# First 32 heads of a sliding-window attention and feed-forward kernel: head pairs on halves of the matrix array, a new step table

## The chip, the cores and the metric

One core of a Trainium2 chip. The metric is the device time of one execution in microseconds (us); of several runs the median counts. A profile is one further execution, with the hardware profiler on.

## The reference

Attention over 4 batches, 8 heads, 768 rows and 64 columns, in which a row sees the last 128 keys and the first 4 ("sinks"), then a feed-forward layer of 3072 tokens:

```python
keep = is_sink | in_window                      # window 128, n_sink 4
scores = np.where(keep, scale * (q @ k.T), -1e9)
a = softmax(scores)
x = (a @ v).transpose(0, 2, 1, 3).reshape(3072, 512)
h = x @ w_in                                    # 512 -> 2048
out = (h * np.cos(h)) @ w_out                   # 2048 -> 512
```

Inputs are fp32; the result must be close to fp32 exactness.

## The kernel before

**Dense part.** The 3072 tokens are cut into six dense pairs of 512 rows, and each pair into 16 slots of 128 hidden columns. A slot is two half products `h_pair` (L476, 12 matmuls of 128x512), the cosine factor on ACT (`half_sine`, `square`) and DVE (`gate_square`, L498, called the gate below), a split of the result into a high and a low part (`g_hi` ACT L507, `g_lo` DVE L514), and `out_pair` (L523, 12 matmuls). Every fp32 product is three matmuls of high and low parts. The last accumulator of the last pair is scaled in two halves, one on ACT (L543), one on DVE (L545).

**Weights.** The arrays come with 64 bits per element. 32 pieces of 512 KB are loaded into two `raw` buffers, and each is put together on DVE by three operations (shift L595, top L601, low L607), rounded on ACT (L628), and its rest is taken on DVE (L631).

**Attention.** Heads 0 to 31 are *early*: the first 256 rows of each batch for 8 heads, in true fp32 matmuls, which the profile records twice each. For two heads at a time q and k are loaded (`load_natural`, L947), transposed on PE into `qk` (L955) and copied out. Before, q went into `early`, where each head's 64 rows are followed by zeros on the other 64 partitions, by two copies of 64x256, so that each head's scores (L992) contract over all 128 partitions. The mask (DVE L1070) and the exponential (ACT L1079) follow, `norm` (L1099, L1097) divides, the probabilities are transposed (`tp`, L1170) and copied (L390 on ACT, L392 on DVE). The values (L1215) multiply by a V that is padded with 64 zero columns, so that two heads are added into one bank. For heads 0 to 15 the sum is split into `xhi` (ACT L349) and `xlo` by a matmul that subtracts (`x_minus`, L354) and a copy. Heads 0 to 15 are done before the first dense slot; heads 16 to 31 and all *late* heads (32 to 95, high and low parts, L1048 scores, L1239 values) lie between dense slots.

**What sets the order.** Class `Plan` takes each step with its engines, duration, dependences and a wished time made from the table `C`, and writes one in-order list per engine. A step with more engines goes to one of them by the same table. `FILL` matmuls without use (L1556, `idle`) are put in where the plan sees PE idle ahead of the first dense matmul. Loads go through SP's queue, two weight pieces and the two scalars through ACT's.

Of the kernel before, what the change touches and what calls it, by code (L numbers as in the profile page):

```python
# [11 lines left out]
I32 = mybir.dt.int32  # L12
# [7 lines left out]
GR = 96 + 2 * NSINK  # L20
# [11 lines left out]
    "POOLF": 0.999, "POOLPEN": 2.492, "R": 2, "RAW": 2, "SAME": 0.056, "SEM": 0.352, "SPE": -0.019, "STEP": 7.601,  # L32
# [140 lines left out]
def attn_moe_kernel(ctx, tc, q, k, v, n_sink, window, w_in, w_out, out):  # L173
# [51 lines left out]
    neg, quarter = neg3[:, 0:2], neg3[:, 2:3]  # L225
# [7 lines left out]
    def setup():  # L233

        nc.scalar.dma_start(out=nw_i[:, 0, :], in_=n_sink.unsqueeze(0))
        nc.scalar.dma_start(out=nw_i[:, 1, :], in_=window.unsqueeze(0))
        nc.gpsimd.memset(ident, 0.0)
# [5 lines left out]
        nc.gpsimd.iota(rc_i[:, 1], pattern=[[1, P]], base=0, channel_multiplier=0)  # L243
        nc.vector.memset(ones, 1.0)
# [11 lines left out]
        nc.vector.tensor_copy(out=rc, in_=rc_i)  # L256
        nc.vector.tensor_single_scalar(out=env.below, in_=rel, scalar=0.0, op=ALU.is_lt)
# [94 lines left out]
    def x_minus(y, p, cs):  # L352
        def fn(e):
            nc.tensor.matmul(  # L354
                out=y.f(p, cs), lhsT=minus, rhs=xhi[:, p, cs], start=False, stop=True, skip_group_check=True
            )
        return fn

    def x_lo(y, p, cs, early):
        def fn(e):  # L360
            if early:
                copy(e, xlo[:, p, cs], y.f(p, cs))
            else:
                e.tensor_tensor(out=xlo[:, p, cs], in0=y.f(p, cs), in1=f32(xhi)[:, p, cs], op=ALU.subtract)
        return fn

    def split_early(plan, x, y, p, t):

# [3 lines left out]
        m = add([("PE", 0.12)], x_minus(y, p, cs), [i], t + 0.3)  # L372
        env.minus.users.append(m)
        j = add([("ACT", act(NT, False)), ("DVE", dve(NT))], x_lo(y, p, cs, True), [m], t + 0.6)
        y.parts[p] += [i, j]
        return [i, m, j]

    def split_late(plan, y, p, t):

        add = plan.add  # L380
        cs = slice(0, PT)
        i = add([("ACT", act(PT))], x_hi(y, p, cs), [k for x in y.xs for k in x.sums[p]] + [y.bx[p // 2]], t)
        j = add(sub(PT), x_lo(y, p, cs, False), [i, y.bx[p // 2]], t + 0.3, port=True)
        y.parts[p] += [i, j]
        for b in y.bf[p // 2]:
            b.users += [i, j]
# [151 lines left out]
    def out_half(y, j, half):  # L538
        def fn(e):
            y.o[j] = f32(raws[y.bo[j].nth]).rearrange("p n w -> p (n w)")[:, :DM]  # L540
            cs = slice(half * DM // 2, (half + 1) * DM // 2)
            if e is nc.scalar:
                e.activation(out=y.o[j][:, cs], in_=y.acc[j][:, cs], func=AF.Copy, scale=-2.0)  # L543
            else:
                e.tensor_single_scalar(out=y.o[j][:, cs], in_=y.acc[j][:, cs], scalar=-2.0, op=ALU.mult)  # L545
        return fn

# [13 lines left out]
    def sub(n):  # L561
        return (("POOL", 0.16 + n * 2.08e-3), ("DVE", dve(n)))
# [198 lines left out]
    def dense_pair(plan, y, s, t, T, w_in_ready, w_out_ready, banks, h_bank):  # L761
# [25 lines left out]
        for j in range(NJ):  # L787
            d = [a5, a6] + w_out_ready[s] + (accs[j].users[:1] or [accs[j]])
# [7 lines left out]
        for j in range(NJ):  # L796
# [7 lines left out]
            elif j < NJ - 1:  # L804
                i = [add(c[:1], out_scaled(y, j, other), d, c0 + 10.0)]
            else:
                i = [add([(e, w / 2)], out_half(y, j, n), d, c0 + 10.0) for n, (e, w) in enumerate(c)]
# [12 lines left out]
    def banded_path(ctx2):  # L820
# [33 lines left out]
        def x1r():  # L854

            if env.x1r is None:
                env.x1r = ap.tile([P, NP * NT], F32R, name="x1r", tag="x1")
                env.vs = env.x1r.rearrange("p (a b c d) -> p a b c d", a=NP, b=2, c=2)
            return env.x1r

        def sink_values():
            x1r()
# [13 lines left out]
        def load_batch_v(o):  # L876
            def fn(e):
                o.vs32 = xb[:, : 2 * D].rearrange("p (n d) -> p n d", d=D)
                for h in range(4):
                    for dup in range(2):  # L880
                        r0 = h * 32 + dup * 8
                        nc.sync.dma_start(
                            out=o.vs32[r0 : r0 + 8], in_=v[o.b, h::4, 0:NSINK, :].rearrange("p s d -> s p d")
                        )
# [36 lines left out]
        def load_v(o):  # L921
            def fn(e):
                if o.early:
                    o.vp = env.vp[o.odd]
                    o.v32 = o.vp[:, :, o.odd * D : o.odd * D + D]
                else:
                    o.v32 = v32s[:, o.bxv.nth, : o.nkb]
# [3 lines left out]
                )  # L931
            return fn
# [9 lines left out]
        def load_natural(tile, src, n):  # L942

            def fn(e):
                dst = tile.rearrange("p a b -> p (a b)")[:, : n * 2 * D].rearrange("p (n h d) -> p n h d", n=n, d=D)
                for h in range(2):
                    nc.sync.dma_start(out=dst[:, :, h, :], in_=src(h).rearrange("(n s) d -> s n d", s=P))  # L947
# [19 lines left out]
        def early_q(e):  # L967
            env.early = ap.tile([P, 2, 4 * P], F32, name="early", tag="ph")
            env.tqe = env.early[:, 1].rearrange("p (a n) -> p a n", a=2)
            for odd in range(2):  # L970
                e.memset(env.tqe[64 - odd * 64 : 128 - odd * 64, odd], 0.0)

        def early_v(e):
            env.vp = [
                ap.tile([P, CB, 2 * D], F32, name="vpe", tag="vr"),
                v32_t[:, : CB * 2 * D].rearrange("p (n d) -> p n d", d=2 * D),
            ]
            e.memset(env.vp[0][:, :, D:], 0.0)
            e.memset(env.vp[1][:, :, :D], 0.0)

        def k_out(o):
            def fn(e):
                o.tk = ap.tile([P, o.nkb, o.sw], F32, name=f"tk_{o.tag}", tag="tk")
                copy(e, o.tk.rearrange("p n s -> p (n s)"), o.qk[:, 1, : o.nkb * P])
            return fn

        def scores_pe(o, oe, j):
            def fn(e):
                i, w = o.i0 + j, o.ws[j]
                o.s_ps[j] = ps.tile([P, BW], F32, name=f"s_{o.tag}_{j}", tag=o.s_tag[j])  # L990
# [890 lines left out]
```

## Time and profile before

| | |
|---|---|
| runs | 724.87, 725.13, 725.80 us, median 725.13 |
| profiled execution | 727.14 us |
| its span, first to last instruction | 725.3 us |
| PE, DVE, ACT, POOL busy | 98%, 83%, 73%, 18% |
| mean granted clock of PE | 0.998 |
| first dense matmul | 57.08 us |
| gate of slot 0, gate of slot 16 | 69.74 us, 190.75 us |
| last weight subtraction (L631) | 160.0 us |

Busy means that an instruction of the engine is in progress. Matmuls overlap: a dense matmul is recorded with some 390 ns, but the next starts 230 ns after it, so starts tell more than busy times.

### The profile page before, as it was taken

What the parts mean: (1) busy time and instruction counts of PE and PEld (TensorE: products, weight loads), DVE (VectorE), ACT (ScalarE), POOL (GpSimd) and SP (SyncE); (2) the same over time, 40 slices, a digit from 0 to 9 for tenths busy, and PEclk for the clock granted to TensorE, in tenths of its full rate; (3) what the DMA queues carried; (4) which work ended last, traced back from release to release, by engine and by line L of the source; (5) the groups of instructions that cost most, each with busy time, mean ns of one, the idle gap of its engine ahead of it and who ended that gap; (6) DMA issues with size and microseconds to landing.
All of it is one profiled execution on the core that took longest, in us unless ns stands there. A gap on an engine that the chain in (4) does not pass through costs nothing.

```text
span 725.3 us, 12983 instructions
## 1 busy us (share of the span) xinstructions
PE 707.8 (98%) x3674; PEld 583.6 (80%) x3674; DVE 599.3 (83%) x1850; ACT 527.3 (73%) x1344; POOL 127.0 (18%) x213
## 2 busy tenths in 40 slices
PE   7888999999999999999999999999999999999997
PEld 6766787888888888888888888888888888888885
DVE  6889999998988978988978989888988875567763
ACT  3796886787797697796686886877887856566652
POOL 1010000000333222232231232232122322100000
PEclk9999999999999999999999999999999999999999
DMA  5665565533255333355433254533244410375651
GB/s 144 177 181 162 140 178 148 155 67 66 63 118 130 86 67 54 64 125 128 93 58 59 42 144 101 122 63 62 44 124 107 111 35 12 96 198 158 167 138 63
DMA packets 236500, 77.11 MB, mean 106 GB/s; under 512 B 221060, under 2 KB 221060, under 8 KB 236420
## 3 DMA queue, kind: packets, MB, share of 16 engines
q1 hardware_dynamic: 236128, 75.15, 43.5%
q10 hardware_dynamic: 292, 1.05, 0.5%
q8 instruction: 31, 0.51, 0.3%
q14 instruction: 49, 0.40, 0.2%
HBM read 69.86 MB, written 6.29 MB: 105 GB/s over the span
## 4 chain that ended last, share of the span: by engine, by line
PE 78%; ACT 12%; DVE 5%; issue 2%; DMA 2%; SPq 0%; ACTq 0%; DVEq 0%
PE h L476 30%; PE acc L523 30%; PE av L1239 4%; PE s L1048 4%; ACT p L1079 3%; PE s L992 2%; PE tp L1160 2%; PE av L1215 2%; DMA xk<-in_k_dram 2%; ACT p L1097 1%; ACT L485 1%; ACT L1079 1%; PE qk L955 1%; PE tp L1170 1%; ACT early L390 1%
## 5 line engine op out<-in xcount | busy, mean ns | idle before, releaser
L523 PE MATMUL acc<-whi_out,ghi 128*128 128x512 f32 x376 | 158.7, 422 | 0.0
L476 PE MATMUL h<-xhi,whi_in 128*128 128x512 f32 x384 | 155.3, 405 | 0.0
L476 PE MATMUL h<-xlo,whi_in 128*128 128x512 f32 x384 | 150.9, 393 | 0.0
L476 PE MATMUL h<-xhi,wlo_in 128*128 128x512 f32 x384 | 150.1, 391 | 0.0
L523 PE MATMUL acc<-whi_out,glo 128*128 128x512 f32 x376 | 147.8, 393 | 0.0
L523 PE MATMUL acc<-wlo_out,ghi 128*128 128x512 f32 x376 | 147.1, 391 | 0.0
L1198 POOL TENSOR_SCALAR_AFFINE_SELECT ph<-ph 128x512 fp32r<-128x512 f32 x128 | 87.2, 681 | 230.9 <-DVE ph L1191 227.1
L485 ACT ACTIVATE r<-h 128x512 f32<-128x512 f32 x96 | 57.1, 598 | 47.9 <-PE h L476 45.3
L476 PEld LDWEIGHTS h<-xlo,whi_in 128*128 128x128 f32 x384 | 72.1, 188 | 16.2
L523 PEld LDWEIGHTS acc<-whi_out,glo 128*128 128x128 f32 x376 | 70.6, 188 | 15.8
L476 PEld LDWEIGHTS h<-xhi,whi_in 128*128 128x128 f32 x384 | 72.3, 188 | 12.0 <-DVE r L498 0.3
L476 PEld LDWEIGHTS h<-xhi,wlo_in 128*128 128x128 f32 x384 | 72.5, 189 | 11.3
L523 PEld LDWEIGHTS acc<-whi_out,ghi 128*128 128x128 f32 x376 | 71.4, 190 | 10.4
L1079 ACT ACTIVATE p<-p,st 128x136 f32<-128x136 f32 (+1 forms) x192 | 79.3, 415 | 0.3
L523 PEld LDWEIGHTS acc<-wlo_out,ghi 128*128 128x128 f32 x376 | 71.3, 190 | 9.2
L498 DVE SCALAR_TENSOR_TENSOR r<-r,h 128x512 f32<-128x512 f32 x96 | 64.5, 674 | 16.9 <-ACT r L491 16.3
L507 ACT CAST ghi<-r 128x512 fp32r<-128x512 f32 x94 | 58.2, 619 | 19.6 <-PE acc L523 12.7
L514 DVE TENSOR_TENSOR glo<-r,ghi 128x512 fp32r<-128x512 f32 x94 | 65.3, 694 | 5.6 <-ACT ghi L507 4.9
L1070 DVE CUSTOM_DVE_ANT_0 p<-s,mk 128x136 f32<-128x136 f32 (+1 forms) x192 | 59.7, 313 | 6.2 <-PE s L992 2.8
L1008 ACT CAST l<-tq 64x256 fp32r<-64x256 f32 x64 | 25.8, 403 | 46.9 <-PE s L1048 46.4
L1056 DVE COPY_PREDICATED s<-mk,s 128x128 f32<-128x128 int32 x128 | 37.2, 291 | 25.6 <-PE s L1048 23.7
L1048 PEld LDWEIGHTS s<-r,l 128*128 128x128 f32 x256 | 46.4, 188 | 12.3 <-DVE ph L1191 1.4
(161 smaller groups left out, 1314.7 us busy)
## 6 DMA issues: line engine op xcount, KB each, us to landing
xk<-in_k_dram SPq DMA_DIRECT2D x256, 48.0 KB
raw<-in_moe_w_out_dram SPq DMA_DIRECT2D x16, 512.0 KB
wt<-in_moe_w_in_dram SPq DMA_DIRECT2D x32, 256.0 KB
raw<-in_moe_w_in_dram SPq DMA_DIRECT2D x14, 512.0 KB
v<-in_v_dram SPq DMA_DIRECT2D x64, 96.0 KB
raw<-in_v_dram SPq DMA_DIRECT2D x32, 192.0 KB
out_dram<-wt SPq DMA_DIRECT2D x22, 256.0 KB
wt<-in_moe_w_out_dram SPq DMA_DIRECT2D x20, 256.0 KB
```

The source lines that it names most:

```text
L476: nc.tensor.matmul(out=o.h, lhsT=w[:, c, fs], rhs=xx[:, c, :], start=(c == 0 and n == 0), stop=(c == NC - 1 and n == 2),)
L485: nc.scalar.activation(out=o.r, in_=o.h, func=AF.Sin, scale=0.5)
L498: nc.vector.scalar_tensor_tensor(out=o.r, in0=o.r, scalar=0.5, in1=o.h, op0=ALU.subtract, op1=ALU.mult)
L507: nc.scalar.copy(out=o.ghi, in_=o.r)
L514: e.tensor_tensor(out=o.glo, in0=o.r, in1=f32(o.ghi), op=ALU.subtract)
L523: nc.tensor.matmul(out=y.acc[j], lhsT=gg[:, j * P : (j + 1) * P], rhs=w[:, f, :], start=(f == 0 and n == 0), stop=(f == NFT - 1 and n == 2),)
L1048: nc.tensor.matmul(out=o.s_ps[j][:, :w], lhsT=o.l[:, j * P : (j + 1) * P], rhs=r.rearrange("p n s -> p (n s)")[:, c0 : c0 + w], start=(n = ...
L1056: nc.vector.copy_predicated(out=o.s_ps[j][:, :P], mask=below.bitcast(I32), data=o.s_ps[j][:, SW : SW + P])
L1070: nc.vector.tensor_tensor_reduce(out=o.pj[j][:, :w], in0=o.s_ps[j][:, :w], in1=masks[min(o.i0 + j, 2)][:, :w], op0=ALU.add, op1=ALU.min, s ...
L1079: nc.scalar.activation(out=o.pj[j][:, :w], in_=o.pj[j][:, :w], func=AF.Exp, bias=o.lead.st[:, 0, o.nth, j : j + 1], scale=-1.0, accum_out= ...
L1198: nc.gpsimd.affine_select(out=ph[:, :, b, :], in_=f32(ph)[:, :, 1, :], pattern=[[0, 2 * CB], [(-1, 1)[b], P]], compare_op=(ALU.is_gt, ALU. ...
L1239: nc.tensor.matmul(out=dst, lhsT=lhs, rhs=rhs, start=(n == 0), stop=(n == len(seq) - 1), skip_group_check=True)
```

## The change

- **Scores.** One step per pair of heads: q of both heads lies on 128 partitions (one copy of 128x256), and each head's matmul contracts over its own 64 partitions and row half of the array, into a bank of its own. The four matmuls of a pair stand together, the two heads in turn.
- **Values.** One step per pair: V has 64 columns per head, and each head's matmul uses one column half of the array, into its own half of the partitions of one bank. The zero fills of `early` and V are gone.
- **Split.** `x_minus` is gone; `xlo` is a DVE subtraction of 128x256.
- **Start.** q of the first two heads is loaded ahead of all weights on SP's queue, k on ACT's; the first two weight pieces follow, one on each queue.
- **Sinks.** The sink columns of four late heads are spread to 64 columns; the sink rows of V come by 8 broadcast loads of 32 partitions per batch instead of 8 of 8, and take three DVE operations per head group instead of two.
- **Others.** The two halves of the last accumulator are one operation on ACT. q, k and V of the early pairs have two buffers each. A subtraction of over 256 columns may no longer go to POOL.
- **Table.** Every constant of `C` that shapes the order is new; `FILL` is 110 instead of 60, `WARM` 3 instead of 5.

```diff
-    "L": 1, "LAG": 3.569, "LEAD": 43.095, "NM": 3.042, "NW": 2.459, "NWF": 0.527, "PB": 5, "PEN": 23.912,
+    "L": 1, "LAG": 2.866, "LEAD": 31.596, "NM": 0.567, "NW": 2.085, "NWF": 1.648, "PB": 5, "PEN": 132.787,
...
-        nc.scalar.dma_start(out=nw_i[:, 0, :], in_=n_sink.unsqueeze(0))
+        nc.sync.dma_start(out=nw_i[:, 0, :], in_=n_sink.unsqueeze(0))
         nc.scalar.dma_start(out=nw_i[:, 1, :], in_=window.unsqueeze(0))
+        for e, load in zip((nc.sync, nc.scalar), env.boot):
+            load(e)
...
-        for raw, src in env.first:
-            nc.scalar.dma_start(out=raw.rearrange("p n w -> p (n w)"), in_=src)
+        for e, (raw, src) in zip((nc.scalar, nc.sync), env.first):
+            e.dma_start(out=raw.rearrange("p n w -> p (n w)"), in_=src)
...
-    def x_lo(y, p, cs, early):
-        def fn(e):
-            if early:
-                copy(e, xlo[:, p, cs], y.f(p, cs))
-            else:
-                e.tensor_tensor(out=xlo[:, p, cs], in0=y.f(p, cs), in1=f32(xhi)[:, p, cs], op=ALU.subtract)
+    def x_lo(y, p, cs):
+        def fn(e):
+            e.tensor_tensor(out=xlo[:, p, cs], in0=y.f(p, cs), in1=f32(xhi)[:, p, cs], op=ALU.subtract)
...
-        def q_out(o, odd):
-            def fn(e):
-                r = slice(odd * 64, odd * 64 + 64)
-                copy(e, env.tqe[r, odd], o.qk[r, 0])
-            return fn
...
+        def q_out(o):
+            def fn(e):
+                o.tq = env.tqe[o.btq.nth]
+                copy(e, o.tq, o.qk[:, 0])
+            return fn
...
+                for j in range(CB):
+                    for o in pair:
+                        r = slice(o.odd * 64, o.odd * 64 + 64)
+                        c0 = max(o.i0 + j - 1 - o.kb0, 0) * o.sw
+                        nc.tensor.matmul(
+                            out=o.s_ps[j], lhsT=oe.tq[r, j * P : (j + 1) * P],
+                            rhs=oe.tk.rearrange("p n s -> p (n s)")[r, c0 : c0 + o.ws[j]], start=True, stop=True,
+                        )
+            return fn
```

**PE, from its first transposes on.** `qk` are transposes of q or k, `s` the scores of a head (batch, chunk and head in its name), `idle` the matmuls without use. Before:

```order
L955 MATMUL qk_0_0_167<-ident,xk 128x128 x2
L1556 MATMUL idle<-gt 128x256 x8
L992 MATMUL s_0_0_0_193<-tk_0_0_185,early 128x128
L992 MATMUL s_0_0_1_199<-tk_0_0_185,early 128x256
L1556 MATMUL idle<-gt 128x256 x3
L992 MATMUL s_0_1_0_209<-tk_0_0_185,early 128x128
L1556 MATMUL idle<-gt 128x256 x7
L992 MATMUL s_0_1_1_230<-tk_0_0_185,early 128x256
```

and now:

```order
L945 MATMUL qk_0_0_167<-ident,xk 128x128 x2
L1532 MATMUL idle<-gt 128x256 x6
L974 MATMUL s_0_0_188<-early_153,early_152 128x128
L974 MATMUL s_0_1_189<-early_153,early_152 128x128
L974 MATMUL s_0_0_188<-early_153,early_152 128x256
L974 MATMUL s_0_1_189<-early_153,early_152 128x256
L1532 MATMUL idle<-gt 128x256 x17
L945 MATMUL qk_0_2_225<-ident,xq 128x128 x2
```

The four scores of a pair moved together, and the unused matmuls behind them became more.

**SP's queue at the start.** `xq` and `xk` are q and k of two heads (two loads each), `raw` weight pieces, `vpe`, `v` and `early` are V. Before, with both first weight pieces on ACT's queue:

```order
L947 DMA xq<-in_q_dram 128x2x64 x2
L947 DMA xk<-in_k_dram 128x2x64 x2
L928 DMA vpe<-in_v_dram 128x2x64
L928 DMA v_76<-in_v_dram 128x2x64
L947 DMA xq<-in_q_dram 128x2x64 x2
```

and now, with the first k and one weight piece on ACT's queue:

```order
L235 DMA nw_i<-in_n_sink_dram 1x2
L930 DMA xq<-in_q_dram 128x2x64 x2
L250 DMA raw_71<-in_moe_w_in_dram 128x1024
L911 DMA v_76<-in_v_dram 128x2x64 x2
L911 DMA early_154<-in_v_dram 128x2x64 x2
L930 DMA xq<-in_q_dram 128x2x64 x2
```

The first k left this queue, a weight piece came onto it, and four loads of V stand ahead of the second pair's q instead of two.

**DVE around the last weight subtraction.** `wlo_out` is the rest of a weight piece, `r_12` and `glo_11` belong to the dense slots 12 and 11, `st` ends a mask. Before:

```order
L514 TENSOR_TENSOR glo_11_1790<-r_11_1720,ghi_11_1774 128x512
L1056 COPY_PREDICATED s_0_2_1_0_1787<-mk_101,s_0_2_1_0_1787 128x128
L1021 STREAM_TRANSPOSE tk_0_2_2_1805<-xk_75 128x3x128
L1070 ISA p_0_2_1_1808,st_0_2_0_1745<-s_0_2_1_0_1787,mk_101 128x136
L1070 ISA st_0_2_0_1745 128x1
L631 TENSOR_TENSOR wlo_out_92<-wt0_72,whi_out_91 128x512
L498 SCALAR_TENSOR_TENSOR r_12_1785<-r_12_1785,h_12_1712 128x512
L631 TENSOR_TENSOR wlo_out_92<-wt1_73,whi_out_91 128x512
```

and now:

```order
L593 SCALAR_TENSOR_TENSOR wt1_73<-raw1_71,wt1_73 128x512
L1052 ISA p_0_2_2_1836,st_0_2_0_1697<-s_0_2_2_0_1818,mk_101 128x136
L1052 ISA st_0_2_0_1697 128x1
L494 SCALAR_TENSOR_TENSOR r_13_1773<-r_13_1773,h_13_1720 128x512
L1038 COPY_PREDICATED s_0_2_2_1_1840<-mk_101,s_0_2_2_1_1840 128x128
L617 TENSOR_TENSOR wlo_out_92<-wt1_73,whi_out_91 128x512
```

The last subtraction moved behind the gate of slot 13; before it stood behind that of slot 12.

Counted in the whole lists: ahead of the gate of slot 0, DVE has 3 shifts, 3 tops, 2 lows, 1 subtraction L631, 1 square, 1 mask, 8 copies of 64x256, 1 of 128x384 and 2 casts of 128x256 fewer than before, and 1 normalization of 128x256, 2 operations of 128x1 and 8 subtractions of 128x256 (`xlo`) more. Between the gates of slots 0 and 16 it has 3 shifts, 3 tops, 2 lows, 2 subtractions L631, 1 square, 4 copies of 128x384 and 4 operations on sink rows more, and 7 copies of 64x256, 4 of 128x128, 1 of 128x256, 11 normalizations and some ten operations of late heads fewer. On PE, between the h products of slots 0 and 16, three dense matmuls, six scores of late heads, four transposes and one `x_minus` are fewer; the values of 18 early heads stand there before and now, and the scores of 15 before and 16 now. Behind slot 16 the same three, six and four are more. All 110 `idle` matmuls stand ahead of the first dense one, as did the 60, and seven of the eight `x_minus` did.

## Rows read from the trace of the kernel before

**Rows 1.** The page, part 4: the chain that ended last, by engine.

```profile
PE 78%; ACT 12%; DVE 5%; issue 2%; DMA 2%; SPq 0%; ACTq 0%; DVEq 0%
```

**Rows 2.** Windows: stretch, length, busy us of each engine, clock, DMA share, GB/s.

```profile
75.00:150.00 75.00, 74.26 (x374) 59.93 (x373) 70.32 (x184) 58.76 (x149) 0.00 (x0) 1.00 0.55 153
625.00:650.00 25.00, 25.00 (x112) 20.70 (x111) 13.90 (x26) 14.18 (x24) 0.00 (x0) 1.00 0.66 171
```

**Rows 3.** Waits of PE, 57 to 175 us: total, times, longest.

```profile
PE s L992 <- DVE tk L392: 0.9, 1, 0.9
PE s L992 <- ACT tk L390: 0.8, 2, 0.5
PE av L1215 <- ACT early L390: 0.7, 2, 0.4
PE s L992 <- DVE st L1070: 0.4, 1, 0.4
```

**Rows 4.** Chain of 0 to 60 us: start, length, what.

```profile
2.32 5.88 DMA xk<-in_k_dram
8.99 1.71 PE idle L1556 x8
...
22.11 3.18 DMA xk<-in_k_dram
...
43.42 3.85 DMA xk<-in_k_dram
```

**Rows 5.** Groups by line and shape, 0 to 58 us: count, busy us, mean ns, idle before.

```profile
L595 DVE TENSOR_SCALAR wt<-raw 128x512 int32<-128x512 int32 x11 | 4.6, 419 | 2.3 <-DMA raw<-in_moe_w_in_dram 2.2
L392 DVE COPY early<-qk 64x256 f32<-64x256 f32 x6 | 2.5, 425 | 3.3 <-ACT tk L390 1.7 <-PE qk L955 1.0 <-ACT early L390 0.6
L392 DVE COPY early<-tp 128x384 f32<-128x384 f32 x3 | 1.7, 553 | 0.0
L1099 DVE TENSOR_SCALAR p<-p,st 128x256 f32<-128x256 f32 x7 | 2.2, 349 | 0.0
```

**Rows 6.** Timeline of DVE at three places: start, length, instruction.

```profile
11.38 0.69 DVE L607 SCALAR_TENSOR_TENSOR wt<-raw,wt 128x512 int32<-128x512 int32 x1
12.02 0.42 DVE L1070 CUSTOM_DVE_ANT_0 p<-s,mk 128x256 f32<-128x256 f32 x1
...
69.74 0.68 DVE L498 SCALAR_TENSOR_TENSOR r<-r,h 128x512 f32<-128x512 f32 x1
...
190.75 0.65 DVE L498 SCALAR_TENSOR_TENSOR r<-r,h 128x512 f32<-128x512 f32 x1
```

**Rows 7.** Timeline of PE around two early groups in the dense stretch.

```profile
95.41 0.82 PE L1215 MATMUL av<-early,vpe 128*128 128x256 f32 x4
95.99 0.48 PE L476 MATMUL h<-xhi,whi_in 128*128 128x512 f32 x1
...
97.45 0.59 PE L992 MATMUL s<-tk,early 128*128 128x256 f32 x2
97.88 0.38 PE L1170 MATMUL tp<-ident,p 128*128 128x128 f32 x2
```

**Rows 8.** Timeline of PE around the values of a late head.

```profile
270.08 0.52 PE L1239 MATMUL av<-ph,vr 128*128 128x128 f32 x5
270.44 0.45 PE L476 MATMUL h<-xhi,whi_in 128*128 128x512 f32 x1
270.72 0.39 PE L476 MATMUL h<-xhi,wlo_in 128*128 128x512 f32 x1
270.95 0.40 PE L476 MATMUL h<-xlo,whi_in 128*128 128x512 f32 x1
```

**Rows 9.** Timelines of ACT and DVE at the end.

```profile
719.16 0.60 ACT L533 ACTIVATE raw<-acc 128x512 f32<-128x512 f32 x1 [0.76 <-PE acc L523]
720.51 0.38 ACT L543 ACTIVATE raw<-acc 128x256 f32<-128x256 f32 x1 [0.76 <-PE acc L523]
...
721.01 0.42 DVE L545 TENSOR_SCALAR raw<-acc 128x256 f32<-128x256 f32 x1 [6.60 <-ACT raw L543]
```

More of the change, by code (lines that the diff above doesn't have):

```diff
@@ L561, in sub @@
     def sub(n):
-        return (("POOL", 0.16 + n * 2.08e-3), ("DVE", dve(n)))
+        return (("POOL", 0.16 + n * 2.08e-3), ("DVE", dve(n)))[n > NT :]
     def dma(n):
@@ L879, in fn @@
                 for h in range(4):
[L880 to L884, printed above, removed]
+                    for n in range(2):
+                        src = v[o.b, n * 4 + h, 0:NSINK, :].unsqueeze(0).broadcast_to([4, NSINK, D])
+                        nc.sync.dma_start(out=o.vs32[h * 32 : h * 32 + 32, n, :], in_=src)
             return fn
@@ L931, in fn, with load_v_pair @@
                 )
+            return fn
+        def load_v_pair(o):
+            def fn(e):
+                o.v32 = env.ve[o.bxv.nth].rearrange("p (n h d) -> p n h d", h=2, d=D)
+                for n in range(2):
+                    nc.sync.dma_start(
+                        out=o.v32[:, :, n, :],
+                        in_=v[o.b, o.h + n, o.kb0 * P : (o.kb0 + o.nkb) * P, :].rearrange("(n s) d -> s n d", s=P),
+                    )
             return fn
@@ L1250, in fn @@
             def fn(e):
[L1251 to L1252 removed]
+                copy(e, x.y.f(o.pair, slice(x.n * NT, x.n * NT + NT)), x.f[o.pair])
             return fn
@@ L1362, in before_softmax @@
-                    i = add(dma(2), load_natural(xk_t, src, o.nkb), [bx], pk, lat=2.4 if g else 1.9)
+                        [("ACT", act(NT, False)), ("DVE", dve(NT))], q_out(o), [i, o.btq] + (early[:2] if g == 0 else []),
+                        t - 6 * T + C["EQ"] + 0.6,
+                    )
+                    bb.users.append(q0)
+                    bx, o.btk = buf("xk", 1), buf("tke", 2)
+                    src = lambda c: k[o.b, o.h + c, o.kb0 * P : (o.kb0 + o.nkb) * P, :]
+                    load = load_natural(xk_t, src, o.nkb)
@@ L1430, in softmax @@
             lead = group[0][1]
[L1431 removed]
+            t = head_time(group[0][0]) - (len(group) - 4) * T - T + 3.9 + C["EX" if lead.early else "DX"]
             ready = [i for _, o in group for i in o.msk]
[L1433 to L1438 removed]
+            ex = []
+            for n, (_, o) in enumerate(group):
+                o.nm = [
+                    add(
+                        [("ACT", act(o.w[j]) + (0.0 if o.early else 0.19))], expo(o, j), ready, t + 1.02 * n + 0.01 * j,
+                        table="exp",
+                    )
+                    for j in range(CB)
+                ]
+                ex += o.nm
             t += 1.02 * (len(group) - 1) + 0.5
@@ new lines, in after_softmax @@
+            if o.early:
+                if o.odd == 0:
+                    return
+                pair = oe, _ = heads[g - 1], o
+                te = head_time(g - 1)
+                oe.bxv, bpt = buf("ve", 2), buf("phi", 1)
+                hold = [early[2:], [early_end]][g // 2] if g < 4 else []
+                v0 = add(dma(2), load_v_pair(oe), [oe.bxv, *hold], te - 2 * T + C["EV"] + 3.2, lat=2.4)
+                ready = [v0]
+                for m, w in enumerate(pair):
+                    pt = buf(w.tp_tag, 1)
+                    p0 = add([("PE", 0.107 * o.n)], turn_early(w), w.nm + [pt], head_time(g - 1 + m) + C["EA"] + 1.3)
+                    w.bp.users.append(p0)
+                    both = [("ACT", act(o.n * P, False)), ("DVE", dve(o.n * P))]
+                    p1 = add(both, p_out(w), [p0, ready[1] if m else bpt], head_time(g - 1 + m) + C["EA"] + 1.8)
+                    pt.users.append(p1)
+                    ready.append(p1)
+                bav = buf(oe.av_tag, 1)
+                y0 = add([("PE", 0.84)], values_pair(pair, x), [*ready, bav], te + C["EA"] + 5.0)
+                for bb in (oe.bxv, bpt, *early[2:]):
+                    bb.users.append(y0)
@@ L1640, in banded_path @@
             waiting.append((g, o))
-            if behind:
-                after_softmax(*behind.pop(0))
+            if behind and (behind[0][1].comb or o.odd != o.comb):
+                for _ in range(1 if behind[0][1].comb else 2):
+                    after_softmax(*behind.pop(0))
             if len(waiting) == o.nq:
```

381 lines of the change are left out of this document (158 added, 223 removed), and 13 rows, old and new, of the table C.

## The prediction, made before the changed kernel had run

> **What bounds the kernel now.** I read the chain of work that ended last first: three quarters of it are PE [rows 1]. That is a mean over stages with different limits, so the windows come next. From 75 to 150 us PE is busy 74.26 of 75 us, but DVE 70.32 of 75, that is 94% [rows 2]. From 625 to 650 us PE is full and DVE has 11 us of 25 to spare. So there are two stages, and the border is the end of the weight preparation at 160 us. Behind it PE alone sets the time. Ahead of it PE has no room (all its waits between 57 and 175 us come to 2.8 us [rows 3]), and DVE is so near its own limit that taking work off PE buys only what DVE lets through. A third stage is the one before the first dense matmul at 57.08 us: there the chain runs through three waits for k, 5.88, 3.18 and 3.85 us, and through matmuls without use, such as 8 in 1.71 us [rows 4]. The gate of slot 0 on DVE at 69.74 us and that of slot 16 at 190.75 us [rows 6] are the marks by which I cut the run: 69.7 us, then 121.0 us, then the rest.
>
> **The price of an early group on PE.** Four matmuls of one head's values take from 95.41 to 95.99 us, 0.58 us, and the dense matmul behind them is 0.08 late, so 0.66; the 256-column part of a head's scores takes from 97.45 to 97.88, 0.43 us [rows 7], and the 128-column part half of that, again 0.66 together. If the two halves of the array work at the same time, each pair of heads saves 0.66 on scores and 0.66 on values. No row of before shows two halves at work, so the saving lies between nothing and 0.66 for each. I take the whole for the sum, because PE does not bind there afterwards, as the next part shows.
>
> **Slot 0 to slot 16.** PE loses half of 18 heads' values (18 x 0.33 = 5.9), 15 x 0.66 - 16 x 0.33 = 4.6 on scores, and by the order three dense matmuls (0.7: a dense one starts 0.23 after the last, from 270.72 to 270.95 [rows 8]), six late scores (0.9 as an estimate: 5 matmuls of 128 columns take 0.36, from 270.08 to 270.44 [rows 8], and these have twice the columns), four transposes (0.4, a quarter of 0.43 each) and one `x_minus` (0.2). That is 12.7 us, and 108.3 of 121.0 remain. DVE's work does not fall. Added are 3 shifts (0.42), 3 tops and 2 lows and 2 subtractions and 1 square (0.69 each, as L607), 4 copies of 128x384 (0.55) and 4 small operations on sink rows (bounded by 0.1 and 0.42; 0.35 taken, nearest the normalization): 1.3 + 5.5 + 2.2 + 1.4 = 10.4. Removed are 7 copies of 64x256 (0.425), 5 other copies (0.3 to 0.42), 11 normalizations (0.28 to 0.35) and ten operations of late heads (0.3 to 0.6): 3.0 + 1.7 + 3.4 + 3.5 = 11.6 [rows 5, 6]. The difference of 1 us is within the error of such a sum; I take nothing. DVE then has 0.94 x 121.0 = 113.5 us of work as before, and PE 108.3: DVE becomes the bound. Its idle share of 6% (7.5 us) is time in which it waited for PE, ACT and loads. Waits for PE get shorter, those for weights and ACT do not, so I give back a third: **-2.5 us**, with 0 and -7.5 as bounds.
>
> **Up to the gate of slot 0.** PE gains 7 pairs of values, 8 of scores and 7 `x_minus`, some 11 us, and the 50 additional unused matmuls, at 0.21 each (8 in 1.71) at most 10.5 us, go where the plan saw it idle. So PE is no shorter by itself, but it does not bind here. DVE loses 8 copies of 64x256 (3.4), 1 of 128x384 (0.55), 2 casts (0.85), 3 shifts (1.3), 3 tops, 2 lows, 1 subtraction and 1 square (0.69 each: 4.8), a mask (0.35), and gains a normalization (0.35), two one-column operations and 8 subtractions for `xlo` (the trace has none of 128x256 from PSUM; by the copy of that size on the same engine, 0.425, bounds 0.3 and 0.69: 3.4). Net -7.4 by durations. Instructions overlap, as L607 lasts 0.69 and the next starts 0.64 after it [rows 6]; with a tenth off it is **-6.7 us**. ACT falls by a few us as well. The four weight pieces thus put off fall due between slots 0 and 16, where they are already counted. The bounds are 0, if the waits for k hold the stretch, and -10, if the first of them also shrinks: k of the first pair comes ahead of two weight pieces now. I do not count on that, since the first mask on DVE stands behind two shifts that need both first weight pieces, in either order. POOL's lost memsets lie beside all this and cost nothing.
>
> **Behind slot 16.** PE binds, and the same three dense matmuls, six scores and four transposes are to be done there: 0.7 + 0.9 + 0.4 = **+2.0 us** (bounds 1 and 3). The wider sink turn has the same moving columns, and adds nothing. The sink loads are 8 per batch before and after, on SP's queue. The extra DVE work meets the 11 us in 25 that DVE has free [rows 2].
>
> **The end.** Now the two halves of the last accumulator run one after the other, ACT from 720.51, DVE until 721.43. A whole one on ACT takes 0.60, to 721.11 [rows 9]: **-0.3 us**.
>
> **Sum.** -6.7 - 2.5 + 2.0 - 0.3 = -7.5 us. The profiled execution took 727.14 (725.3 of span and 1.8 around it), which gives 719.6; it lay 2.0 above the median of the runs, so against 725.13 I say **717.6 us**.
>
> **Rivals.**
> *Both engines give way.* If DVE's waits between slots 0 and 16 were nearly all for PE, the whole 7.5 us go: 725.13 - 6.7 - 7.5 + 2.0 - 0.3 = 712.6, and 709.3 if the first stretch gives 10. For it: PE's windows are full and nearly all of the chain is PE's. Against: some of DVE's idle time is waiting for weights, 2.3 us before the shifts in the first stretch alone [rows 5].
> *The halves do not overlap.* Then PE saves only 12.7 - 11.2 = 1.5 us (with one head's scores more inside), 119.5 of 121.0 remain, and the middle term is -1.5 at best, say -1: 719.1. Half of the gain of the split would be gone and hardly be seen, since the first term is DVE's.
> *The first stretch keeps its length.* k and q have one load buffer each as before, so that the next load waits for the last transposes; the three waits, 12.9 us in all [rows 4], may stay, and the additional unused matmuls stand in line ahead of q and k transposes. Then -2.5 + 2.0 - 0.3 = -0.8: 724.3, no change that can be told.
> *Slower: each half waits until the other has left the array.* Place: the four matmuls of a group, in 17 groups between slots 0 and 16. Price: a matmul lasts 0.39 to 0.40 while the next starts after 0.23 [rows 8]; without that overlap each of 68 matmuls costs 0.16 more, 10.9 us. PE then needs 119.5 + 10.9 = 130.4, the middle term is +9.4, and the sum 725.13 - 6.7 + 9.4 + 2.0 - 0.3 = 729.5. It decides from a price of about 0.1 a matmul on (119.5 + 68 x 0.1 = 126.3, +5.3, against -5.0 of the others). Against it: the late values switch between 64 and 128 columns five times in 0.36 us, and the dense matmul behind them is 0.05 late in all (0.28 for 0.23 [rows 8]). But no row has halves of the rows.
> The Trainium skill, TensorEngine Tiling (Array Packing), Key Properties, says that a change of the tiling mode, not of the tile, drains the engine. By that, going in and out of halves would cost at two places in a group, but not between the halves: 17 x 2 x 0.16 = 5.4 us as an estimate, which the 12.7 us of room would hide if the halves overlap, and which would give 723.9 or so if they do not. The trace has such changes of mode in the late values, at no more than 0.05 us. The same page, Theoretical Speedup, gives up to 2 times for a contraction of 64, which is the upper bound used above; no run here shows it yet.
>
> **How the numbers follow.** Forecast 0.45, both engines 0.17, no overlap 0.16, same first stretch 0.10, drain 0.12. The predicted time is that of the likeliest. The range 708.5 to 724.5 takes in the first three and half of the fourth, about 0.83, less a little at the low end. A change of 0.2% (1.4 us) is about what this kernel's measurement can tell from none. Below 723.7 lie the first three: 0.78. The unchanged stretch is the same: 0.10. The drain is slower: 0.12.
>
> **What the profile after would show.** The first dense matmul near 50 us and the gate of slot 0 near 63 say that the first term is right; at 69 or later it is wrong. The gate of slot 16 should come near 181, with DVE busier than 94% and PE's waits in the windows from 65 to 150 well above 2.8 us; PE full and DVE at 94% would mean that the halves do not overlap. On PE's timeline a pair's scores should take 0.66 instead of 1.32 us. The stretch behind slot 16 should be 2 us longer. Wrong would be the prediction, above all, if the waits for k still come to 12 us ahead of the first dense matmul, or if the new step order has ACT or DVE wait for each other where the lists only seem to be shorter.

## The result, and the profile after

The changed kernel takes 733.49 us (median of 4 runs, 731.41 to 735.27), the kernel before 725.35 in the same session: ratio 1.0111, with an interval of 1.0096 to 1.0126. It is 1.1% slower; the forecast was 717.6, faster by 1%. The profiled execution took 735.27, of which 733.5 are span, 1.8 above its median as the one of before was. One execution of a run below, 792.63 us at a granted clock of 0.85 against 0.992 and more in its others, is left out of that run's times.

DVE's timeline at the two marks, the gates of slots 0 and 16 (start, length, instruction; L494 is now the line of the gate):

```profile
63.09 0.69 DVE L494 SCALAR_TENSOR_TENSOR r<-r,h 128x512 f32<-128x512 f32 x1
...
184.79 0.67 DVE L494 SCALAR_TENSOR_TENSOR r<-r,h 128x512 f32<-128x512 f32 x1
```

They stood at 69.74 and 190.75 [rows 6], and the last matmul began at 720.09 us before and begins at 728.08 now. So the three stretches are:

| stretch | before | after | change | forecast |
|---|---|---|---|---|
| start to gate of slot 0 | 69.7 | 63.1 | -6.6 | -6.7 |
| to gate of slot 16 | 121.0 | 121.7 | +0.7 | -2.5 |
| to the last matmul | 529.3 | 543.3 | +14.0 | +2.0 |
| last matmul to the end of the span | 5.2 | 5.4 | +0.2 | -0.3 |

The whole loss is behind slot 16, in work that the halves of the array do not touch. The chain that ended last, by engine, is the first thing that shows it, against [rows 1]:

```profile
PE 62%; ACT 15%; DVE 12%; DMA 4%; issue 4%; SPq 1%; POOL 0%; ACTq 0%; DVEq 0%
```

PE had 78% of it. Next come the waits of PE behind slot 16 (engine, line, what it waited for: total, times, longest), now:

```profile
PE gp L1128 <- DVE gc L1115: 4.7, 5, 1.1
PE h L472 <- DVE r L494: 3.3, 2, 3.1
PE s L1030 <- DVE st L1052: 2.8, 4, 1.2
PE cs L690 <- DVE col L683: 1.3, 1, 1.3
PE s L1030 <- DVE ph L1167: 0.3, 1, 0.3
PE tp L1140 <- DVE st L1052: 0.3, 1, 0.3
```

and the same question to the kernel before, from 186 us on:

```profile
PE tp L1160 <- DVE st L1070: 0.9, 4, 0.2
```

12.7 us against 0.9: the 11.8 us more are nearly the 12 by which that stretch missed its forecast. All are waits for DVE, which is no busier than before over the whole run (599.8 us against 599.3), though more of its work now lies between the gate of slot 16 and the last matmul (439.7 us against 430.1, 81% of that stretch in both). It does the same work later than PE asks for it: the sink turn (`gp`) waits for the sink columns (`gc`) five times, a product `h` waits for a gate, scores (`s`) wait until a mask has freed the bank. The longest, at 301.67 us, read on DVE's timeline and then PE's:

```profile
299.77 0.21 DVE L1101 CAST vs<-yt 32x128 fp32r<-32x128 f32 x1
...
302.96 0.29 DVE L1103 TENSOR_TENSOR vs<-vs,yt 32x128 fp32r<-32x128 f32 x1
303.28 0.69 DVE L489 TENSOR_TENSOR r<-r 128x512 f32<-128x512 f32 x1
304.01 1.28 DVE L494 SCALAR_TENSOR_TENSOR r<-r,h 128x512 f32<-128x512 f32 x2
```

```profile
304.75 0.50 PE L472 MATMUL h<-xhi,whi_in 128*128 128x512 f32 x1 [3.08 <-DVE r L494]
```

The twelve operations on the sink rows of one batch stand in a row ahead of two gates; PE stands for 3.08 us. How much of this is theirs is not shown: ACT's square for one of the two gates (L487) ended only at 302.38 us.

On the halves of the array, PE's timeline around the scores of a pair:

```profile
129.75 0.40 PE L519 MATMUL acc<-whi_out,glo 128*128 128x512 f32 x1
130.08 0.93 PE L974 MATMUL s<-early 64*128 64x128 f32 x8
130.94 0.49 PE L519 MATMUL acc<-whi_out,ghi 128*128 128x512 f32 x1
131.27 0.39 PE L519 MATMUL acc<-wlo_out,ghi 128*128 128x512 f32 x1
```

From 130.08 to 130.94 is 0.86 us for two heads, where the prediction had 0.66. The dense matmul before the group and the first one behind it each take 0.33 instead of 0.23 until the next start. So a group costs about 1.06 us, against 1.32 before [rows 7]: 0.26 saved, not 0.66. That is 0.4 us more than the 0.65 that one head's columns take by [rows 7]. The Trainium skill, TensorEngine Tiling (Array Packing), Key Properties, has the engine drain when the tiling mode changes; the trace agrees, with these 0.4 us a group for going in and coming out, though it does not show that they are a drain.

### The profile page after: what moved, and what is told of

Its sections match the earlier page's. It is cut to its first block, busy times and chain, and to the rows that moved or that the text cites. A ratio compares the mean times of both kernels' runs of the same rounds, so it can differ in the third digit from the quotient of the medians.

```text
span 733.5 us, 13021 instructions
## 1 busy us (share of the span) xinstructions
PE 702.3 (96%) x3712; PEld 565.2 (77%) x3712; DVE 599.8 (82%) x1830; ACT 521.0 (71%) x1319; POOL 144.3 (20%) x230
## 4 chain that ended last, share of the span: by engine, by line
PE 62%; ACT 15%; DVE 12%; DMA 4%; issue 4%; SPq 1%; POOL 0%; ACTq 0%; DVEq 0%
PE acc L519 24%; PE h L472 23%; ACT p L1061 4%; PE av L1212 4%; PE s L1030 4%; ACT p L1079 2%; ACT L481 1%; DMA raw<-in_v_dram 1%; PE idle L1532 1%; PE tp L1149 1%; PE s L974 1%; PE tp L1140 1%; PE av L1187 1%; DVE p L1052 1%; ACT r L481 1%
## 5 line engine op out<-in xcount | busy, mean ns | idle before, releaser
L519 PE MATMUL acc<-whi_out,ghi 128*128 128x512 f32 x376 | 154.5, 411 | 0.0
L1174 POOL TENSOR_SCALAR_AFFINE_SELECT ph<-ph 128x512 fp32r<-128x512 f32 x128 | 89.7, 701 | 201.3 <-DVE ph L1167 191.6
L494 DVE SCALAR_TENSOR_TENSOR r<-r,h 128x512 f32<-128x512 f32 x96 | 64.7, 677 | 14.4 <-ACT r L487 14.0
L1030 PE MATMUL s<-r,l 128*128 128x264 f32 x256 | 55.3, 297 | 6.1 <-DVE st L1052 3.3
```

What stands on the lines that cost most here:

```text
L494: nc.vector.scalar_tensor_tensor(out=o.r, in0=o.r, scalar=0.5, in1=o.h, op0=ALU.subtract, op1=ALU.mult)
L519: nc.tensor.matmul(out=y.acc[j], lhsT=gg[:, j * P : (j + 1) * P], rhs=w[:, f, :], start=(f == 0 and n == 0), stop=(f == NFT - 1 and n == 2),)
L1030: nc.tensor.matmul(out=o.s_ps[j][:, :w], lhsT=o.l[:, j * P : (j + 1) * P], rhs=r.rearrange("p n s -> p (n s)")[:, c0 : c0 + w], start=(n = ...
L1174: nc.gpsimd.affine_select(out=ph[:, :, b, :], in_=f32(ph)[:, :, 1, :], pattern=[[0, 2 * CB], [(-1, 1)[b], P]], compare_op=(ALU.is_gt, ALU. ...
```

## The experiments

Times are medians with the granted clock of the profiled execution; marks are read on DVE's timeline as above. Theory A: the step order behind slot 16 costs the time. Theory B: the changed code itself costs it, the wider sinks above all.

**Tables exchanged.** In the first run the new code has the old values of all shared constants, in the second the old code the new ones, in the third the new code the old values of those that place late heads and dense slots. A cut of the first run's edit:

```diff
-    "L": 1, "LAG": 2.866, "LEAD": 31.596, "NM": 0.567, "NW": 2.085, "NWF": 1.648, "PB": 5, "PEN": 132.787,
...
+    "HB": 1.252, "TH2": 7.345, "GA": 16, "GHI": 2, "GLO": 2, "L": 1, "LAG": 3.569, "LEAD": 43.095, "NM": 3.042, "NW": 2.459,
+    "NWF": 0.527, "PB": 5, "PEN": 23.912, "POOLF": 0.999, "POOLPEN": 2.492, "R": 2, "RAW": 2, "SAME": 0.056, "SEM": 0.352, "SPE": -0.019,
...
```

> The changed code with every constant that both tables share set back to its old value (FILL 60 and WARM 5 too); only the new constants of the early pairs stay. Theory A (the step order behind slot 16 costs the time): the stretch from the gate of slot 16 to the end, 548.7 us in the changed kernel against 534.5 before, comes back to 535 to 538; with a gate of slot 16 near 185 that gives 718 to 724. Theory B (the changed code itself, sinks above all, costs it): the stretch stays at 545 or more, and the time at 730 or more.

> The old code with every shared constant at its new value (FILL 110 and WARM 3 too). Theory A: the stretch behind the gate of slot 16 is longer than 540 us here as well, and PE waits there for DVE; with a first part no shorter than before, 735 us or more. Theory B: the stretch stays within 2 us of 534.5.

> The changed kernel with only those constants set back that place late heads and dense slots (DA, DH, DM, DQ, DS, DV, DX, LAG, NM, T, HO, SX, CK, CV, CL, CR, CT, CS, CE, ZV, VP); those of the first part, of the weights and of the choice between engines stay new. Theory A, if it is the placing: behind slot 16 at most 538 us, and 718 to 724 in all. Theory A', if it is the choice between engines (POOL against DVE): 545 us or more behind slot 16. Theory B: 545 or more as well.

Measured: 759.68, 746 to 749 and 748.84 us; from the gate of slot 16 to the end 568.5, 554.4 and 566.9 us. The second fell as Theory A has it. The first and third meet, by the letter, the bound that was set for Theory B (545 or more) and miss that of Theory A, but as 18 to 20 us more than the changed kernel's 548.7 they are no return to anything: the old constants do not bring back the old order under the new code. So these two decide nothing. A table is no carrier of an order, since the planner makes the order from the table together with the code's durations and dependences. To exchange the order itself, it had to be written out.

**Orders exchanged.** The order was written out as a list of steps with their engines (`REST`), and put in place of the planner's from slot 16 on.

```diff
+REST = """
...
         steps = plan.order(True)
+        names = dict(P="PE", A="ACT", G="POOL", D="DVE", S="SP")
+        rest = [(int(w[:-1]), names[w[-1]]) for w in REST.split()]
+        kept_out = {id(plan.steps[i][1]) for i, _ in rest}
+        steps = [step for step in steps if id(step[2]) not in kept_out]
+        steps += [(0.0, n, plan.steps[i][1], e) for n, (i, e) in enumerate(rest)]
```

> The changed code and its order up to the gate of slot 16; from there on every step in the order, and on the engine, that it had in the kernel before (no step has to move for its dependences; 188 steps change engine, mostly between DVE and POOL; one constant, CR, back to 9.813, so that the checks of weights are as many per slot). Theory A (the order behind slot 16 costs 12 us): the stretch from the gate of slot 16 to the end falls from 548.7 to 535 to 538 us, and the time to 719 to 722. Theory B (the changed code costs it: wider sinks, slower sink loads): the stretch stays at 544 or more and the time at 729 or more.

> The mirror of the last: the old code and order up to the gate of slot 16, from there on the changed kernel's order and engines (CR 11.475). Theory A: the stretch behind the gate grows from 534.5 to 543 to 550 us, and the time to 734 to 740. Theory B: the stretch stays within 3 us of 534.5, the time within 3 us of 726.

Measured, the new code with the old order: gate of slot 16 at 186.24 us, span 723.7, so 537.5 us behind it. The old code with the new order: gate at 190.41, span 737.9, so 547.5 us behind it, and 738.50 in the median. Both stretches are where Theory A put them, and neither where Theory B did. PE's waits behind slot 16, first the new code with the old order, then the old code with the new:

```profile
PE tp L1302 <- DVE st L1214: 2.8, 8, 0.6
PE h L634 <- DVE r L656: 1.2, 1, 1.2
PE tp L1302 <- ACT p L1241: 0.7, 3, 0.2
PE most_t L1814 <- DVE most L1808: 0.2, 1, 0.2
```

```profile
PE gp L1305 <- DVE gc L1292: 4.1, 5, 1.0
PE h L637 <- DVE r L659: 1.8, 1, 1.8
PE s L1209 <- DVE st L1231: 1.3, 2, 1.1
PE av L1400 <- POOL ph L1359: 0.3, 1, 0.3
PE row_t L1843 <- DVE row L1839: 0.2, 1, 0.2
PE cs L865 <- DVE col L858: 0.2, 1, 0.2
```

The waits go with the order: the sink turn's five waits come with the new one, in the old code too. So of 14.2 us behind slot 16 (548.7 against 534.5) 11.2 are the order's by the first run, 13.0 by the second.

Three limits go with these numbers. The list carries the engine of each step too (188 steps change theirs in the first run), so the order and the choice of engines are not told apart. In the first run a part of the 11.2 only moved ahead of the mark, as slots 0 to 16 take 124.9 us there instead of 121.7: from the gate of slot 0 to the end it is 662.3 us against 670.4, or 8.1 less. And the listed waits of PE are only a part of the cost. In the second run they are 7.9 us, 7.0 more than before, out of 13.0; its clock is granted at 0.83 on 310 to 320 us, and for the rest PE counts as busy (533.1 us behind the gate against 528.1 before, with the same matmuls). What these 5 us consist of is not taken apart here.

The time of the first run missed, though. Its profiled execution took 725.39 us at a clock of 1.000, but the four others 729.82 to 732.11 at 0.987 to 0.992, and the median is 730.89. In that execution PE is idle for about a quarter of 140 to 150 us:

```profile
140.00:150.00 10.00, 7.51 (x34) 4.80 (x34) 9.57 (x25) 8.18 (x19) 1.10 (x2) 1.00 0.90 201
```

The kernel before has no such gap there [rows 2]. In other profiles the granted clock falls behind such gaps (below), which would account for the spread; where it fell is not shown, since the timed executions have no profile.

**The two heads of a pair in blocks.**

```diff
-                for j in range(CB):
-                    for o in pair:
+                for o in pair:
+                    for j in range(CB):
...
-                for n, (kb, qs) in enumerate(oe.cols):
-                    for o in pair:
+                for o in pair:
+                    for n, (kb, qs) in enumerate(oe.cols):
```

> The changed kernel with the two heads of an early pair one after the other, in scores and in values, instead of in turn. If the saving (0.86 us for a pair's scores in place of 1.32) comes from neighbouring matmuls on different halves, and each fp32 matmul is two instructions of which only the last and the next head's first meet, the group goes back to 1.2 us or more here: only one of three borders between matmuls is left between halves. If the halves work side by side however they are queued, it stays at 0.9 or less. The whole time is not what this run is for: within 5 us of the changed kernel.

Measured: 733.87 us, and on PE's timeline

```profile
130.36 0.93 PE L974 MATMUL s<-early 64*128 64x128 f32 x8
131.22 0.49 PE L519 MATMUL acc<-whi_out,ghi 128*128 128x512 f32 x1
```

again 0.86 us. The halves overlap wholly, however they are queued. The Trainium skill, TensorEngine Tiling (Array Packing), Key Properties, calls the tiles independent of each other; this run agrees. What is missing from the factor of two is then the way in and out.

**The whole array again.**

```diff
-                        r = slice(o.odd * 64, o.odd * 64 + 64)
+                        r = slice(0, P)
...
-                            out=av[o.odd * 64 : o.odd * 64 + 64, (qs[0] - oe.i0) * P : (qs[-1] + 1 - oe.i0) * P],
-                            lhsT=oe.v32[:, kb - oe.kb0, o.odd], rhs=o.pt[:, oe.offs[n] * P : oe.offs[n + 1] * P],
+                            out=av[:, (qs[0] - oe.i0) * P : (qs[-1] + 1 - oe.i0) * P],
+                            lhsT=oe.v32[:, kb - oe.kb0].rearrange("p h d -> p (h d)"),
...
```

> The changed kernel with the same early steps in the same order, but each matmul of scores and values on the whole array, one head after the other (all 128 partitions are contracted and all 128 columns of V used, so that the two heads of a pair are mixed in the result). By the traces a pair's two groups then cost 0.6 us more on PE (1.32 for about 1.05, twice). If PE counts between the gates of slots 0 and 16, that stretch grows from 121.7 by 3 to 5 us, and the time to 736 to 739. If DVE bounds it, as the prediction has it, it grows by less than 1.5 us and the time stays within 2 us of 733.5.

Measured: 738.81 us, against 733.49 for the changed kernel. The gate of slot 0 is at 67.65 and that of slot 16 at 191.39:

```profile
67.65 0.69 DVE L494 SCALAR_TENSOR_TENSOR r<-r,h 128x512 f32<-128x512 f32 x1
...
191.39 0.67 DVE L494 SCALAR_TENSOR_TENSOR r<-r,h 128x512 f32<-128x512 f32 x1
```

So the gates come 4.6 and 6.6 us later. The first of them has to be read at a like clock. Three kernels have the same code and order up to the gate of slot 0: the changed one, the one with the old order behind slot 16 (above), and the first one of "Both repairs" below. In this order, their windows of 15 to 20 us (clock is the third number from the end):

```profile
15.00:20.00 5.00, 3.68 (x19) 3.04 (x20) 4.03 (x18) 1.41 (x5) 0.00 (x0) 0.68 0.66 195
15.00:20.00 5.00, 3.90 (x33) 3.57 (x34) 4.38 (x19) 2.37 (x7) 0.00 (x0) 1.00 0.65 187
15.00:20.00 5.00, 3.82 (x18) 3.17 (x19) 3.66 (x17) 1.27 (x4) 0.00 (x0) 0.57 0.65 184
```

Their gates of slot 0 are at 63.09 us and at

```profile
61.38 0.68 DVE L656 SCALAR_TENSOR_TENSOR r<-r,h 128x512 f32<-128x512 f32 x1
...
64.39 0.69 DVE L672 SCALAR_TENSOR_TENSOR r<-r,h 128x512 f32<-128x512 f32 x1
```

On 20 to 25 us the third was granted 0.75. The kernel on the whole array had 0.51 and 0.81 in these two windows, much like the third. Against that one the halves are worth 3.3 us ahead of slot 0, where the prediction had credited PE with nothing. Between the gates the whole array costs 2.0 (123.7 against 121.7), more than the one theory's 1.5 and less than the other's 3. At a like clock it would be more, since the changed kernel was granted 0.66 on 145 to 150 us and this run 1.00. Each of these readings is of one execution.

The group itself is a control for the price of the halves, as the array keeps its form here:

```profile
137.29 0.40 PE L519 MATMUL acc<-whi_out,glo 128*128 128x512 f32 x1
137.53 1.47 PE L974 MATMUL s<-early 128*128 128x128 f32 x8
138.65 0.58 PE L519 MATMUL acc<-whi_out,ghi 128*128 128x512 f32 x1
139.06 0.40 PE L519 MATMUL acc<-wlo_out,ghi 128*128 128x512 f32 x1
```

Two heads take 1.12 us until the next start, and the dense matmul behind them 0.41 instead of 0.23. That is 1.30 in all, or twice the 0.65 of one head's columns, with nothing left over.

**Eight operations of DVE less.**

```diff
+        n_piece = env.pieces = getattr(env, "pieces", -1) + 1
...
             def top(e):
+                if n_piece < 8:
+                    return
```

> The changed kernel without the operation top (0.61 us from start to start) in the first eight weight pieces, which leaves the upper bits out of these weights; all else in the same order. If DVE sets the stretch up to the gate of slot 0 and seven or eight of these pieces lie in it, the gate comes 4 to 5 us earlier than at 63.1. If the waits for k and the latencies between engines set it, it stays within 1.5 us of 62 to 63.

Measured: 733.95 us in one run; gate of slot 0 at 60.04, 3.1 us earlier than in the changed kernel, for 4.9 us of DVE work. By the bounds that were set, this lies between the two theories. But the clock was granted at 1.00 here:

```profile
15.00:20.00 5.00, 5.00 (x47) 4.37 (x43) 4.04 (x16) 2.55 (x10) 0.00 (x0) 1.00 0.62 171
...
60.04 0.69 DVE L494 SCALAR_TENSOR_TENSOR r<-r,h 128x512 f32<-128x512 f32 x1
```

Against the run with the old order behind slot 16, which up to this gate differs only by these eight operations and had 1.00 as well, with the gate at 61.38, the gain is 1.3 us: DVE's work counts there for about a quarter. With the run before, both engines lie on the chain of that stretch, PE no less than DVE.

**No matmuls without use.**

```diff
                 if n == 0:
                     env.idle = ps.tile([P, 2, P], F32, name="idle", tag="b1")
+                if n:
+                    return
```

> The changed kernel with one matmul without use instead of 110, all else in the same order. If these matmuls stand on the chain (they are 16% of it up to 60 us, 9 us), the gate of slot 0 comes 2 to 6 us earlier than at 63.1, unless the clock is granted lower for longer. If DVE sets that stretch, as the prediction has it, the gate stays within 1 us of 63.1 at an unchanged clock; with PE less busy the granted clock may stay at half for longer, and the gate come later than 64.

Measured: 733.04 us, gate of slot 0 at 62.14. The 110 matmuls neither cost nor give anything that the time shows; they lie in gaps. The clock fell once in this run's first stretch as well, later (0.95 on the mean of 20 to 57 us; with the matmuls 0.92 on 0 to 20).

**The sink loads later.** The steps of the changed kernel in its own order, written out, with one step moved on SP's queue. What it is about, on SP's timeline of the changed kernel:

```profile
131.14 0.41 SPq L566 DMA_DIRECT2D raw<-in_moe_w_out_dram  x1
131.67 5.82 SPq L861 DMA_DIRECT2D yt<-in_v_dram  x8
137.60 0.39 SPq L566 DMA_DIRECT2D raw<-in_moe_w_out_dram  x1
```

and on DVE's:

```profile
141.73 0.43 DVE L581 TENSOR_SCALAR wt<-raw 128x512 int32<-128x512 int32 x1 [2.44 <-DMA raw<-in_moe_w_out_dram]
```

Eight broadcast loads hold the queue for 5.82 us, the weight piece behind them lands late, and DVE stands for 2.44 us. Then PE stands, and its clock is granted at 0.66 over the next 5 us (145 to 150; clock is the third number from the end):

```profile
145.00:150.00 5.00, 4.77 (x16) 3.40 (x15) 4.02 (x12) 4.71 (x10) 0.52 (x1) 0.66 0.90 200
```

> The changed kernel with one step moved on SP's queue: the eight broadcast loads of the first batch's sink rows (131.7 to 137.5 us, first used at 171) go behind the last weight load. If they hold up the weight piece for which DVE waits 2.4 us at 139.3 us, that wait goes, the gate of slot 16 comes at 181 to 183.5 instead of 184.8, and the time falls by 1.5 to 3.5 us. If DVE or a buffer would have been late anyway, the gate stays within 0.7 us of 184.8.

Measured: gate of slot 16 at 182.59, and the wait for the weight piece is gone. Slots 0 to 16 take 120.2 us, 1.5 less, and the clock stays at 1.00 on 145 to 150 us. In the median, 733.13, hardly any of it shows (0.36 us, less than the spread of the runs), so the time missed its 1.5 to 3.5; in the profiled execution the clock is granted at 0.83 on 300 to 310 us instead, where the changed kernel had 1.00.

**Both repairs, and the old order for all.** The first joins the moved sink loads and the old order from slot 16 on, the second gives the new code the old order from its first step, with each pair's step where its last single step stood.

> The two repairs together: the changed code and order up to the gate of slot 16, with the first batch's sink loads behind the last weight load, then the old order. If the repairs add up, the gate of slot 16 comes at 183 to 184.5 and the rest takes 532 to 534 to the last matmul, as in the run with the old rest alone: 720 to 723 at a clock of 0.998 or more, some 2 us less than that run's profiled execution (725.4) and 2 to 5 less than before. If the clock is granted lower again in the timed runs (0.987 to 0.992 there), 727 to 730.

> The changed code with all of its steps in the order, and on the engines, of the kernel before, from the first step on (FILL 60, CR 9.813; a step for a pair of heads stands where that of its last matmul stood; some early steps move by a few places for their dependences; the first batch's sink loads stand behind the last weight load). If the early pairs on halves are worth what the run on the whole array shows (6 to 7 us up to the gate of slot 16), and the old order behind slot 16 costs 532 to 534 us, the gate of slot 16 comes at 184 to 187 and the time at 717 to 722. If an order made for single heads delays the pairs (the first head waits for the second), the gate comes at 189 to 193 and the time at 724 to 728. If it is above 730, an order can't be carried from one code to the other at all.

Measured: 728.95 and 755.14 us. The first is in the bounds that were set for a lower clock (0.991 to 0.994 here). In it, 538.7 us lie behind the gate of slot 16, as hoped, but the gate is at 189.39, since the two orders do not meet smoothly: PE is idle for a quarter of 175 to 190 us, and the clock falls behind it:

```profile
175.00:190.00 15.00, 11.44 (x56) 8.39 (x55) 13.09 (x49) 11.24 (x34) 2.19 (x5) 0.99 0.25 42
190.00:195.00 5.00, 4.91 (x18) 4.07 (x19) 3.15 (x9) 1.15 (x2) 1.54 (x3) 0.68 0.62 164
```

In the second, the gate of slot 16 is at 214.8 with long waits of PE for DVE (8.8 us for masks alone), so an order made for single heads does not serve pairs. Behind it are 537.3 us: with the old order there, the new code took 537.3 to 538.7 us in three runs whose first parts differ. None of the twelve kernels beat the kernel before; the nearest is 728.95.

## Why the prediction was wrong

**The step that failed is "Behind slot 16. PE binds".** It counted the work left there (+2.0 us), and took from the kernel before that PE does it without waiting. That PE has no waits there is a property of the old order, not of the stage. The new order has 12.7 us of them, and the two exchanges of the order give 11.2 and 13.0 us of the stretch to it, engines included. None of the rivals was this one. The sentence that came nearest, a step order in which engines wait for each other "where the lists only seem to be shorter", stood at the end without a price. Which places of the new order cost how much is shown only by PE's waits; they were not undone one by one.

The count of +2.0 does not hold at the mark either. The three dense matmuls were counted from h product to h product in PE's list, but the stretches were cut at DVE's gates. From gate to gate PE does 189 matmuls of `out_pair` now instead of 181, and behind the gate of slot 16 it has nine fewer left. That the new code with the old order needs 537.5 us there, 3.0 more than the old code, is therefore near the forecast by luck: PE's waits alone grow by 4.0 (4.9 against 0.9).

**Up to the gate of slot 0: -6.6 for -6.7,** but the number is partly luck and the reason the smaller part of it. At a clock of 1.00 on 15 to 20 us the same code and order reach this gate at 61.38, 8.4 us earlier than before. The prediction let DVE alone set this stretch and put PE's relief at nothing. At like clocks, taking away 4.9 us of DVE work moved the gate by 1.3, and giving back the halves moved it by 3.3. A third cause was not tested: PE's waits for k ahead of the first dense matmul, 4.4 us before, no longer stand in the list of its waits. Where the chain began with a load of k [rows 4], it now begins with a weight piece (6.94 us from 2.30 on).

**Slots 0 to 16: +0.7 for -2.5.** Two terms were mis-sized. The saving of PE is 0.26 us a group as read on scores, not 0.66, so that 17 groups give 4.4 us instead of 11.2. And the sink loads, taken as equal because they are eight per batch before and after, occupy SP for 0.62 us each instead of 0.30 (medians), which made a weight piece late; without that the stretch is 120.2. That DVE bounds it, so that PE's relief is only partly paid out, is not shown: the whole array costs 2.0 us there, and more at a like clock, for 17 groups of 0.26. Nor did DVE become busier there than the 94% that the prediction named as a sign: it was busy for 111.2 of 121.7 us, after 111.6 of 121.0 before (91% and 92%; the 94% in the sum is that of 75 to 150 us).

**The drain between the halves** did not come; going into the halves and out costs about 0.4 us a group at its two ends. The late values, which the prediction took for such changes, show no such price (at most 0.05 us [rows 8]); whether their 64 columns change the array's mode at all is not shown. **The end** went as forecast from matmul to copy: two whole copies on ACT end at 729.11, 1.03 us after the start of the last matmul, against 1.34; the last store took the gain back.

## What to carry to other kernels

Where an order is chosen anew, the stage that the edit does not touch is at risk too: "this engine binds here" is true of an order, and the waits of that engine in the new order are a term of the sum with a price. A loss can be given to code or to order by exchanging the written-out order, with its engines, between the two kernels; exchanging the constants that made it shows nothing. A mark that the clock shifts has to be compared with a run at the same clock. Loads of one count are not loads of one price: look up how long each holds its queue, and what waits behind it.

## What the hardware showed that was not expected

- Matmuls of two heads on different halves of the array start 7 ns apart when queued in turn, and 13 ns apart when those of one head are queued ahead of all of the other's: 0.86 us for a pair in either order.
- Going into and out of the halves costs about 0.4 us for each group: 0.33 instead of 0.23 us at the dense matmul on each side and 0.2 within. A group on the whole array has nothing of the kind (1.30 us for two heads, twice 0.65).
- A broadcast load of 32 partitions holds SP's queue for 0.62 us, one of 8 partitions without broadcast 0.30.
- Behind gaps of PE the granted clock fell to half for a few us (0.50 on 18 to 20 us in the changed kernel, 0.66 on the mean of 145 to 150, 0.68 on 190 to 195 in the run of both repairs), and not behind every one: the run with the old order behind slot 16 kept 1.00 in its profiled execution with PE as busy on 10 to 15 us as in the changed kernel (3.68 of 5 us against 3.71), and ran at 0.987 to 0.992 in others, 4 to 7 us longer.
- Up to the gate of slot 0, the same code and order took 61.38 us with 1.00 granted on 15 to 25 us, 63.09 with 0.68 and 0.98 on the two halves of it, and 64.39 with 0.57 and 0.75.
